# The last 64 tokens of q and k, both heads in one bank, on quarters of the TensorE array

## The chip, the cores and the metric

The kernel runs on one core of one Trainium2 chip. The metric is the device time of one execution in microseconds; a kernel's time is the median of several executions. The profile is one execution, recorded by the hardware. Its engines are PE (TensorE, the matrix array; PEld is its loading of weights), DVE (VectorE), ACT (ScalarE), POOL (GpSimd) and SP (SyncE, which here issues DMAs).

## What is computed

Linear attention, then two feed-forward layers, all in float32. Batch 8, 8 heads, 576 tokens, head size 64, 128 features.

```python
def phi(x):
    proj = np.einsum('bhsd,df->bhsf', x, w_phi)
    proj = proj - np.max(np.abs(proj), axis=-1, keepdims=True)
    return np.concatenate([np.exp(proj), np.exp(-proj)], axis=-1)
q_p, k_p = (phi(q), phi(k))
kv = np.einsum('bhsf,bhsd->bhfd', k_p, v)
z = np.sum(k_p, axis=2)
num = np.einsum('bhsf,bhfd->bhsd', q_p, kv)
den = np.einsum('bhsf,bhf->bhs', q_p, z)[..., None] + 1e-06
x = num / den
...
xk = mu_k * x + (1.0 - mu_k) * x_prev        # xr alike, with mu_r
k = np.maximum(xk @ w_k, 0.0)
x = 1.0 / (1.0 + np.exp(-(xr @ w_r))) * (k * k @ w_v)
...
h = np.maximum(x @ w_in, 0.0)                # then a convolution over 3 tokens
out = h * gate @ w_out                       # gate: sigmoid of the convolution
```

## The kernel before

Attention works on pairs of heads: 8 x 4 = 32 pairs, each with q and k of two heads, head 0 on SBUF partitions 0 to 63 and head 1 on 64 to 127 (tile `rqk`). The 576 tokens of a head are four groups of 128 and a rest of 64. In `rqk` the last 64 columns of q stand right ahead of the last 64 of k, so that one slice of 128 columns holds both rests.

`block(Pi)` (L388) runs once for each pair, in a software pipeline. It does `turn` and `turn_end` for pair Pi (transposes of the centred projections of q, and their exponentials `qf`), `front` for pair Pi + 2 (the projections of the rest of q and k, `rows_last`, and of the rest of k, `rows4`, tile `pk`, with their centring), the projections of q for pair Pi + 1 (`rows4`, tile `pq`), `sums4` (kv and z, tile `pkv`), `results` (tile `pn`, divided into `xn`), and `features` for pair Pi + 2 (the exponentials of k: `kp`, and `kr` for the rest). The output of a pair is transposed into `xT` by `column` (tile `px`) and `column_end` (tile `pr`, which it shares with the transposes of `turn_end`).

Before the change the rest goes so. `rows_last` (L263) takes two PSUM tiles (in the program `p1`, in the trace `p`), one for each head, and makes one product for each: 64 rows of the array (the head's half), 128 columns of weights (the 64 tokens of q, then the 64 of k), 128 features streamed through. `centre` (L282) is a reduce (`mx<-p`) and a subtraction (`t<-p,mx`) on DVE for each head. In the result q's tokens are on partitions 0 to 63 and k's on 64 to 127, so `features` takes `t[64:]` of each head to the head's half of `kr` with four ACT operations, and `turn_end` (L355) transposes the tile of each head, of which it uses the 64 columns of q.

The trace names a matmul's tile as rows*columns of the array: 64*128 for `p`, `pk` and `pq`, 128*64 for `pkv` and `pn`, 128*128 for transposes and the feed-forward products. A float32 product is two passes there, each with its own weight load; a transpose and a float32r product is one.

The order on PE is written out by hand; that of DVE and ACT is set by a scheduler with a model of the timeline. From Pi = 4 (`MS`) on, parts of the first feed-forward layer (`moe`: `psk`, `psr`, `psv`) are put between the blocks on PE; from Pi = 5 the block begins with `px`. After the last pair follow the rest of that layer and the second one (`psh`, `pso`). In the first blocks DVE also rounds the feed-forward weights from float64 (`h`, with an ACT operation ahead).

PSUM has eight banks: a ring of three (`psm`, tag `mm`), from which `rows_last`, part of `pq` and the feed-forward products allocate, and a ring of five (`psa`, tag `at`).

Of the kernel before, what the change touches and what calls it, by code (L numbers as in the profile page):

```python
# [8 lines left out]
F32 = mybir.dt.float32  # L9
F32R = mybir.dt.float32r  # L10
U32 = mybir.dt.uint32
AF = mybir.ActivationFunctionType
# [3 lines left out]
P = 128  # L16
B, H, S, D = 8, 8, 576, 64
NP = H // 2
DM, DFF, FT = 512, 1024, 128
# [23 lines left out]
def fused_kernel(ctx: ExitStack, tc: tile.TileContext, qk, va, wphi, ones2, mu, wk, wv, wr, win, wout, cw, out):  # L43
    nc = tc.nc
    T, SY = nc.tensor, nc.sync
# [23 lines left out]
    V, A, G = Noted(nc.vector), Noted(nc.scalar), Noted(nc.gpsimd)  # L69
# [31 lines left out]
    ident = const.tile([P, P], F32, name="ident")  # L101
    make_identity(nc, ident)
    wp0 = const.tile([P, 2 * FT], F32, name="wp0")
# [50 lines left out]
    psm = ctx.enter_context(tc.tile_pool(name="psm", bufs=PSM, space=bass.MemoryType.PSUM))  # L154


    with ExitStack() as p1:
        pool = p1.enter_context(tc.tile_pool(name="p1", bufs=1))
# [63 lines left out]
        for h in range(2):  # L222
            for w in ((wr, wrh, wrl), (wv, wvh, wvl)):
                n = w[1].shape[1] // 2
# [10 lines left out]
        xk, vts = {}, {}  # L235
# [18 lines left out]
        ts, kps_, kvs = {}, {}, {}  # L254

        def rows(Pi, prods):

            x = xk[Pi]
            for o, h, j in prods:
                r = slice(D * h, D * h + D)  # L260
                T.matmul(o, x[r, j * P:j * P + P], wp0[r, h * FT:h * FT + FT], start=True, stop=True)

        def rows_last(Pi):  # L263
            ps = [psm.tile([P, 512], F32, tag="mm", name="p1") for _ in range(2)]
            ps = [p_[:, :FT].rearrange("p (a n) -> p a n", a=1) for p_ in ps]
            rows(Pi, [(ps[h][:, 0], h, 4) for h in range(2)])
            t = pool.tile([P, 1, 2, FT], F32, tag="t1", bufs=2, name="t")
            for h in range(2):
                centre(ps[h], t[:, :, h])
            ts[Pi] = [t]  # L270

        def rows4(Pi, j0, nm):
# [9 lines left out]
        def centre(ps, t):  # L282
            n = ps.shape[1]
            mx = pool.tile([P, 4], F32, tag="mx", bufs=3, name="mx")[:, :n]
            V.tensor_reduce(mx, ps, axis=AX.X, op=ALU.max, apply_absolute_value=True)
            V.tensor_tensor(t, ps, mx.unsqueeze(2).to_broadcast([P, n, FT]), ALU.subtract)
# [8 lines left out]
        def features(Pi, tk):  # L295
            kp = kps_[Pi] = []
            for h in range(2):
                k_ = pool.tile([P, 4, 2, FT], F32, tag="kp", bufs=2, name="kp")
                A.activation(k_[:, :, 0], tk[h], AF.Exp)
                A.activation(k_[:, :, 1], tk[h], AF.Exp, scale=-1.0)  # L300
                kp.append(k_)

            k_ = pool.tile([P, 2, FT], F32, tag="kr", bufs=1, name="kr")
            for h in range(2):
                r = slice(64 * h, 64 * h + 64)
                A.activation(k_[r, 0], ts[Pi][0][64:, 0, h], AF.Exp)
                A.activation(k_[r, 1], ts[Pi][0][64:, 0, h], AF.Exp, scale=-1.0)
            kp.append(k_)

        def sums4(Pi):  # L310
# [11 lines left out]
        def column(Pi):  # L322

            xn = xns.pop(Pi)
            xt = main.tile([P, 2 + S], F32, tag="xT", bufs=XT, name="xT")
            xT[divmod(Pi, NP)] = xt
            G.memset(xt[:, 0:1], 0.0)
            px = psa.tile([P, 512], F32, tag="at", name="px")
            for j in range(4):
                T.transpose(px[:, j * P:j * P + P], xn[:, j], ident)  # L330
            A.copy(xt[:, 1:513], px)
            return xn, xt
# [20 lines left out]
            return qf, t1  # L353

        def turn_end(qf, t1, pr):  # L355
            for h in range(2):
                T.transpose(pr[:, P + h * P:2 * P + h * P], t1[:, 0, h], ident)
            for h in range(2):
                for c in range(2):
                    A.activation(qf[h][:, c, 512:], pr[:, P + h * P:P + h * P + 64], AF.Exp, scale=1.0 - 2 * c)  # L360

        def results(Pi, qf):

# [20 lines left out]
        def front(Pi):  # L384
            rows_last(Pi)
            return centre4(rows4(Pi, 5, "pk"), "tk")

        def block(Pi):  # L388
# [4 lines left out]
            if Pi >= 0:  # L393
                if Pi > MS:
                    x = column(Pi - 1)
                qf, t1 = turn(Pi)
                pr = psa.tile([P, 512], F32, tag="at", name="pr")
                if Pi > MS:
                    copies = column_end(*x, pr)
                turn_end(qf, t1, pr)  # L400
                if Pi > MS:
                    copies()
# [15 lines left out]
            if nk:  # L418
                features(Pi + 2, tk)
                if Pi + 2 > 1:  # L420
                    load_v(Pi + 2)
# [175 lines left out]
        with tc.manual_schedule(engines={mybir.EngineType.PE}):  # L597
            tk = front(0)
            features(0, tk)
            for Pi in range(-1, B * NP):  # L600
                for n, _ in enumerate(attention(Pi)):
                    extras(Pi, n)
                    feed(Pi)
            x = column(B * NP - 1)
            column_end(*x, psa.tile([P, 512], F32, tag="at", name="px"))()


    with ExitStack() as p2:
        pool = p2.enter_context(tc.tile_pool(name="p2", bufs=1))
# [88 lines left out]
        for g_ in range(0, B * S, 4 * S):  # L698
            a = g_
# [65 lines left out]
```

## Time and profile before

| | |
|---|---|
| median of 3 executions | 1225.81 us (1225.13 to 1226.35) |
| the profiled execution | 1225.83 us, its span 1224.0 us |
| PE busy | 98% of the span |
| DVE busy | 62% |
| ACT busy | 57% |
| the chain that ended last | PE 90%, DVE 5%, ACT 2% |

A busy share is an average over stages: the profile has to be read stage by stage, as the rows further down do. The chain is followed back from the last instruction, at each step to what released it. The length of a matmul in the trace runs from its start to the end that the recorder models, and neighbours overlap; the pace of a group is read from one group's start to the next one's.

### The profile page before, as it was taken

The page shows a single profiled execution, that of the slowest core. Times are in us where ns is not written, and L with a number is a line of the kernel's source. Part 1 is how long each engine was busy: PE and PEld are TensorE (multiplying, and loading weights), DVE is VectorE, ACT ScalarE, POOL GpSimd, SP SyncE. Part 2 cuts the span into 40 slices and gives each one's busy share as a digit, 9 for nine tenths or more (in the row PEclk, how much of TensorE's full clock was granted, in tenths as well). Part 3 has the DMA queues.
Part 4 walks back from the last instruction along what each step waited for, and adds up shares of the span by engine and source line. Part 5 has one row for each costly group of instructions (what it writes and reads, how often), then busy time and mean ns, then how long its engine had stood idle before and what let it go on. Part 6 is the DMA issues. An engine that isn't in the chain of part 4 may idle for free.

```text
span 1224.0 us, 29034 instructions
## 1 busy us (share of the span) xinstructions
PE 1202.0 (98%) x11920; PEld 1135.5 (93%) x11920; DVE 762.1 (62%) x1584; ACT 696.7 (57%) x1644; POOL 86.3 (7%) x213
## 2 busy tenths in 40 slices
PE   7899999999999999999999999999999999999998
PEld 6787999999999999999999999998889888888887
DVE  7989676576675765766656534426555754466555
ACT  6777765566565655665555533325654655455554
POOL 1000001111111111111000000000000000000000
PEclk9999999999999999999999999999999999999999
DMA  6665121223232322332110004050122101210220
GB/s 223 221 218 196 59 80 59 86 93 120 89 93 76 117 83 86 93 121 71 50 42 23 11 21 158 20 188 19 44 63 63 43 21 62 63 53 11 63 62 32
DMA packets 56532, 100.81 MB, mean 82 GB/s; under 512 B 10320, under 2 KB 38608, under 8 KB 56400
## 3 DMA queue, kind: packets, MB, share of 16 engines
q1 hardware_dynamic: 40272, 61.65, 14.8%
q0 software_dynamic: 6768, 27.69, 7.4%
q10 hardware_dynamic: 9360, 9.61, 2.8%
q8 instruction: 94, 1.54, 0.5%
q14 instruction: 38, 0.31, 0.1%
HBM read 66.42 MB, written 27.26 MB: 77 GB/s over the span
## 4 chain that ended last, share of the span: by engine, by line
PE 90%; DVE 5%; ACT 2%; issue 1%; DMA 1%; SPq 0%; ACTq 0%; DVEq 0%
PE psh L150 5%; PE psh L152 5%; PE psh L151 5%; PE psv L150 5%; PE pkv L318 5%; PE psv L151 5%; PE psk L151 5%; PE psv L152 5%; PE psk L152 5%; PE psk L150 5%; PE pso L150 5%; PE pso L151 5%; PE pso L152 5%; PE pn L371 4%; PE psr L150 3%; PE psr L151 3%
## 5 line engine op out<-in xcount | busy, mean ns | idle before, releaser
L58 DVE SCALAR_TENSOR_TENSOR ct<-h,cw,ct 128x460 f32<-128x460 f32 (+2 forms) x160 | 111.4, 696 | 84.6 <-ACT ct L58 83.5
L150 PE MATMUL psv<-kh,wvl 128*128 128x288 f32 x480 | 142.2, 297 | 0.0
L151 PE MATMUL psv<-kl,wvh 128*128 128x288 f32 x480 | 141.9, 296 | 0.0
L151 PE MATMUL psk<-ml,wkh 128*128 128x288 f32 x480 | 141.7, 295 | 0.0
L152 PE MATMUL psk<-mh,wkh 128*128 128x288 f32 x480 | 141.4, 295 | 0.0
L152 PE MATMUL psv<-kh,wvh 128*128 128x288 f32 x480 | 141.1, 294 | 0.0
L150 PE MATMUL psk<-mh,wkl 128*128 128x288 f32 x480 | 140.9, 294 | 0.0
L152 PE MATMUL psh<-xh,wih 128*128 128x462 f32 (+1 forms) x320 | 118.9, 372 | 0.0
L151 PE MATMUL psh<-xl,wih 128*128 128x462 f32 (+1 forms) x320 | 118.8, 372 | 0.0
L151 PE MATMUL pso<-gl,woh 128*128 128x460 f32 (+1 forms) x320 | 117.9, 370 | 0.0
L152 PE MATMUL pso<-gh,woh 128*128 128x460 f32 (+1 forms) x320 | 117.7, 370 | 0.0
L58 ACT ACTIVATE kf<-psk 128x288 f32<-128x288 f32 x128 | 52.2, 408 | 111.5 <-PE psk L152 105.6
L150 PE MATMUL psh<-xh,wil 128*128 128x462 f32 (+1 forms) x320 | 107.3, 372 | 0.0
L58 ACT ACTIVATE h<-psh 128x462 f32<-128x462 f32 (+3 forms) x128 | 47.8, 409 | 76.8 <-PE psh L152 75.6
L150 PEld LDWEIGHTS psv<-kh,wvl 128*128 128x128 f32 x480 | 90.3, 188 | 0.8
L151 PEld LDWEIGHTS psv<-kl,wvh 128*128 128x128 f32 x480 | 90.4, 188 | 0.0
L150 PEld LDWEIGHTS psk<-mh,wkl 128*128 128x128 f32 x480 | 90.2, 188 | 0.1
L151 PEld LDWEIGHTS psk<-ml,wkh 128*128 128x128 f32 x480 | 90.2, 188 | 0.0
L152 PEld LDWEIGHTS psv<-kh,wvh 128*128 128x128 f32 x480 | 90.2, 188 | 0.0
L152 PEld LDWEIGHTS psk<-mh,wkh 128*128 128x128 f32 x480 | 90.2, 188 | 0.0
L58 ACT ACTIVATE kp<-t 128x512 f32<-128x512 f32 x128 | 70.3, 618 | 34.6 <-PE pkv L318 28.9
L58 DVE SCALAR_TENSOR_TENSOR x<-sg,psv 128x288 f32<-128x288 f32 x64 | 29.0, 454 | 97.5 <-PE psv L152 91.4
(108 smaller groups left out, 2822.7 us busy)
## 6 DMA issues: line engine op xcount, KB each, us to landing
rqk<-qk POOLq DMA_DIRECT2D x29, 576.0 KB, 4.8
va<-va POOLq DMA_DIRECT2D x30, 325.0 KB, 4.8
x2s<-x SPq DMA_DIRECT2D x30, 288.0 KB, 2.3
raw<-wk SPq DMA_DIRECT2D x8, 512.0 KB, 5.4
raw<-wv SPq DMA_DIRECT2D x8, 512.0 KB, 4.0
raw<-win SPq DMA_DIRECT2D x16, 256.0 KB, 2.9
raw<-wout SPq DMA_DIRECT2D x16, 256.0 KB, 2.9
x2r<-x2s ACTq DMA_DIRECT2D x16, 231.0 KB, 2.6
```

Source lines behind the costliest of these rows:

```text
L58: x = op(*a, **k)
L150: T.matmul(ps, wl, xh, start=first, stop=False)
L151: T.matmul(ps, wh, xl, start=False, stop=False)
L152: T.matmul(ps, wh, xh, start=False, stop=last)
L318: T.matmul(o[r:r + 64], k_[:, r:r + 64], v_, start=(i == 0), stop=(i == len(prods) - 1))
L371: T.matmul(pn[b_][64 * r:64 * r + 64, j], qf[h_][:, c, o:o + 64], kv[:, c, h_], start=(j == 0 and c == 0), stop=(j == 4 - b_ and c == 1))
```

## The change

The two products of `rows_last` become four, each for one head and one of q and k (`a` = 0 for q, 1 for k), with 64 rows and 64 columns of the array: head 0 on the quarter at rows 0 and columns 0, head 1 on the quarter at rows 64 and columns 64. All four write one PSUM tile: head h on partitions 64 h to 64 h + 63, q in the first 128 columns, k in the next 128. One reduce and one subtraction centre it. `features` then takes both heads in one operation for each sign, and `turn_end` transposes one tile, in which the heads stand side by side.

```diff
         def rows_last(Pi):
-            ps = [psm.tile([P, 512], F32, tag="mm", name="p1") for _ in range(2)]
-            ps = [p_[:, :FT].rearrange("p (a n) -> p a n", a=1) for p_ in ps]
-            rows(Pi, [(ps[h][:, 0], h, 4) for h in range(2)])
-            t = pool.tile([P, 1, 2, FT], F32, tag="t1", bufs=2, name="t")
-            for h in range(2):
-                centre(ps[h], t[:, :, h])
+            x = xk[Pi]
+            ps = psm.tile([P, 512], F32, tag="mm", name="p1")[:, :2 * FT].rearrange("p (a n) -> p a n", a=2)
+            for a in range(2):
+                for h in range(2):
+                    r = slice(D * h, D * h + D)
+                    T.matmul(ps[r, a], x[r, 512 + D * a:512 + D * a + D], wp0[r, h * FT:h * FT + FT], start=True, stop=True)
+            t = pool.tile([P, 2, FT], F32, tag="t1", bufs=2, name="t")
+            centre(ps, t)
             ts[Pi] = [t]
...
             k_ = pool.tile([P, 2, FT], F32, tag="kr", bufs=1, name="kr")
-            for h in range(2):
-                r = slice(64 * h, 64 * h + 64)
-                A.activation(k_[r, 0], ts[Pi][0][64:, 0, h], AF.Exp)
-                A.activation(k_[r, 1], ts[Pi][0][64:, 0, h], AF.Exp, scale=-1.0)
+            A.activation(k_[:, 0], ts[Pi][0][:, 1], AF.Exp)
+            A.activation(k_[:, 1], ts[Pi][0][:, 1], AF.Exp, scale=-1.0)
             kp.append(k_)
...
         def turn_end(qf, t1, pr):
-            for h in range(2):
-                T.transpose(pr[:, P + h * P:2 * P + h * P], t1[:, 0, h], ident)
+            T.transpose(pr[:, P:2 * P], t1[:, 0], ident)
             for h in range(2):
                 for c in range(2):
-                    A.activation(qf[h][:, c, 512:], pr[:, P + h * P:P + h * P + 64], AF.Exp, scale=1.0 - 2 * c)
+                    A.activation(qf[h][:, c, 512:], pr[:, P + h * D:P + h * D + D], AF.Exp, scale=1.0 - 2 * c)
```

On PE, in the block of Pi = 5 (the first in which `px` comes first), the order is this, - before and + with the change. Sizes are those of the weights and of what streams; `wp_74` is `wp0`, and a row with a number behind `p` is the projection of the rest.

```order
 L330 MATMUL px<-ident,xn 128x128 x4
 L350 MATMUL pt<-ident,t 128x128 x8
 L335 MATMUL pr<-ident,xn 128x128
-L357 MATMUL pr<-ident,t 128x128 x2
-L261 MATMUL p_1366<-wp_74,rqk 128x128
-L261 MATMUL p_1367<-wp_74,rqk 128x128
+L356 MATMUL pr<-ident,t 128x128
+L269 MATMUL p_1332<-wp_74,rqk 64x128 x4
 L261 MATMUL pk<-wp_74,rqk 128x128 x8
 L261 MATMUL pq<-wp_74,rqk 128x128 x8
 L318 MATMUL pkv<-va,kp 64x65 x32
```

The place of each group is as it was; between the transposes and `pk` one transpose less and two products more stand. The other blocks differ in the same rows.

On DVE this is the part of the block of Pi = 1 around the centring of the rest, before the change. `h` is a weight that is being rounded.

```order
L58 TENSOR_SCALAR xn<-pn,rd 128x128
L58 TENSOR_SCALAR h<-h 128x512
L58 TENSOR_REDUCE mx<-p_476 128x1
L58 TENSOR_REDUCE mx<-p_477 128x1
L58 TENSOR_SCALAR h<-h 128x512
L58 TENSOR_TENSOR t<-p_476,mx 128x128
L58 TENSOR_TENSOR t<-p_477,mx 128x128
L58 SCALAR_TENSOR_TENSOR h<-raw,h 128x512
```

The same place with the change:

```order
L58 TENSOR_SCALAR xn<-pn,rd 128x128
L58 TENSOR_SCALAR h<-h 128x512
L58 TENSOR_REDUCE mx<-p_462 128x2
L58 TENSOR_SCALAR h<-h 128x512
L58 TENSOR_TENSOR t<-p_462,mx 128x256
L58 SCALAR_TENSOR_TENSOR h<-raw,h 128x512
```

Two reduces became one with two results, and two subtractions one of twice the columns; the neighbours kept their order. In later blocks a few neighbours changed places on DVE and ACT: a `ml<-xf,mh` stands between the two subtractions of `pq`, and a cast of `mh` between the `kp` operations of the two heads.

## Rows read from the trace of the kernel before

**Rows 1.** The page's busy times and, in 40 slices, the clock granted to TensorE

```profile
PE 1202.0 (98%) x11920; PEld 1135.5 (93%) x11920; DVE 762.1 (62%) x1584; ACT 696.7 (57%) x1644; POOL 86.3 (7%) x213
...
PEclk9999999999999999999999999999999999999999
```

**Rows 2.** Stretches: length; busy PE, PEld, DVE, ACT, POOL (instructions); granted clock, DMA share, GB/s

```profile
35.50:47.20 11.70, 9.49 (x195) 8.44 (x196) 11.63 (x29) 9.27 (x25) 1.07 (x2) 1.00 0.66 216
...
82.00:712.00 630.00, 627.57 (x8010) 611.49 (x8009) 420.98 (x941) 378.70 (x966) 70.46 (x110) 1.00 0.26 83
```

**Rows 3.** What PE waited for from 70 to 740 us: us in total, times, longest

```profile
PE psv L484 <- DVE x L58: 0.7, 1, 0.7
PE pq L261 <- ACT qf L58: 0.7, 1, 0.7
PE pn L371 <- DVE t L58: 0.7, 1, 0.7
PE pk L261 <- ACT xT L58: 0.4, 1, 0.4
```

**Rows 4.** PE in order of time, 420.0 to 424.9 us: start, length to last end

```profile
420.24 0.27 PE L335 MATMUL pr<-ident,xn 128*128 128x128 f32 x1
420.35 0.38 PE L357 MATMUL pr<-ident,t 128*128 128x128 f32 x2
420.66 0.49 PE L261 MATMUL p<-wp,rqk 64*128 64x128 f32 x4
420.98 1.06 PE L261 MATMUL pk<-wp,rqk 64*128 64x128 f32 x16
421.88 1.06 PE L261 MATMUL pq<-wp,rqk 64*128 64x128 f32 x16
422.87 2.09 PE L318 MATMUL pkv<-va,kp 128*64 128x65 f32 x64
```

**Rows 5.** PE at 420.62 to 420.66 us alone, in order of time

```profile
420.45 0.27 PE L357 MATMUL pr<-ident,t 128*128 128x128 f32 x1
```

**Rows 6.** Tile `p` from 82 to 740 us: duration ns min/median/max, first and last start

```profile
L261 PE MATMUL p<-wp,rqk x100: 272/322/373, 83.0 to 666.6; 64*128 64x128 f32 x100
```

**Rows 7.** Tile `pkv` from 420 to 430 us, columns as in rows 6

```profile
L318 PE MATMUL pkv<-va,kp x64: 219/222/271, 422.9 to 424.7; 128*64 128x65 f32 x64
```

**Rows 8.** PE in order of time, 28 to 64 us

```profile
29.95 2.09 PE L318 MATMUL pkv<-va,kp 128*64 128x65 f32 x64
31.86 0.61 PE L318 MATMUL pkv<-va,kr 128*64 128x130 f32 x8
32.31 2.27 PE L371 MATMUL pn<-kvf,qf 128*64 128x65 f32 x72
35.52 1.25 PE L350 MATMUL pt<-ident,t 128*128 128x128 f32 x8 [0.95 <-DVE t L58]
...
38.65 1.25 PE L261 MATMUL pk<-wp,rqk 64*128 64x128 f32 x16 [1.23 <-DVE xn L58]
...
62.01 1.25 PE L261 MATMUL pk<-wp,rqk 64*128 64x128 f32 x16 [1.23 <-DVE xn L58]
```

**Rows 9.** DVE in order of time, 33 to 48 us

```profile
37.75 0.76 DVE L58 TENSOR_TENSOR xn<-pn,rd 128x256 f32<-128x256 f32 x2
38.42 0.34 DVE L58 TENSOR_SCALAR xn<-pn,rd 128x128 f32<-128x128 f32 x1
...
39.01 0.48 DVE L58 TENSOR_REDUCE mx<-p 128x1 f32<-128x128 f32 x2
39.41 0.42 DVE L58 TENSOR_SCALAR h<-h 128x512 uint32<-128x512 uint32 x1
```

**Rows 10.** ACT in order of time, 4 to 26 us

```profile
16.83 1.02 ACT L58 ACTIVATE kr<-t 64x128 f32<-64x128 f32 x4
```

**Rows 11.** DVE in order of time, 4 to 26 us

```profile
10.87 1.29 DVE L58 TENSOR_REDUCE mx<-pk 128x4 f32<-128x512 f32 x2 [0.23 <-PE pk L261]
...
21.16 0.43 DVE L58 TENSOR_SCALAR h<-h 128x512 f32<-128x512 f32 x1 [0.51 <-ACT h L58]
```

## The prediction

> **What bounds the kernel now.** I read the page first: PE is busy 98% of the span and the granted clock stands at the top digit in all forty slices [rows 1]. A busy share does not say that PE never waits, so the table of stretches came next [rows 2]. From 82 to 712 us PE is busy 627.6 of 630 us, DVE two thirds of it, ACT three fifths. There an instruction more or less on PE moves the end by its own length. From 35.5 to 47.2 us it is the other way: DVE works 11.63 of 11.70 us and PE 9.49. The list of what PE waited for between 70 and 740 us [rows 3] has four single waits, 2.5 us in all, each for DVE or ACT. So one edit has two prices: on PE in the long stretch, on DVE in the first 70 us, and what it saves on ACT and DVE after that is worth no more than those four waits.
>
> **What one block costs on PE.** I took the block at 420 us, in order of time [rows 4], and the last transpose of it alone [rows 5]. Each float32 product of the program runs as two passes: two products of `p` give x4, eight of `pk` x16. Passes of head 0 and head 1 use different halves of the array's rows and run as a pair, so `pk` needs 421.88 - 420.98 = 0.90 us for eight pairs, 0.1125 us a pair. `p` has two pairs, 0.225 us, but takes 420.98 - 420.66 = 0.32. The other 0.10 is the first load, which nothing covers: the first matmul of `p` takes 373 ns, later ones 272 [rows 6]. Ahead of it the two transposes start at 420.35 and 420.45, 0.10 to 0.11 apart, but `p` starts 0.21 after the second: a change of tile shape (128*128 to 64*128) holds PE for 0.10. From `pq` to `pkv` (64*128 to 128*64) it is alike: 0.99 us instead of 0.90. There the load is half as wide, and the first matmul takes 271 ns instead of 222, so 0.05 for a first load of 64 columns [rows 7].
>
> **The change, part by part.**
>
> The second transpose of `t1` goes: -0.11 us in a block.
>
> The products of the last tokens go from two to four, on 64 by 64 tiles. Does a quarter tile run faster? The trace has no 64*64 tile, but it has tiles half as wide. In `pkv` 64 passes (32 pairs) over 65 columns take 31.86 - 29.95 = 1.91 us, 0.060 a pair; the eight over 130 columns take 0.45 us, 0.1125 a pair [rows 8]. The load was 64 wide in both, so the columns that stream through set the pace, and all passes here stream 128. Four products are eight passes: four pairs at 0.1125 = 0.45 us if the two heads still run together (+0.225), eight single passes = 0.90 us if they don't (+0.675). I take the pairs: pairs on different columns of the array that share a bank (`pkv`) are in the trace, and so are pairs on different rows with a bank each (`pk`). The new pair differs in both, and nothing in these rows says that it must queue.
>
> Tile shapes: 128*128 to 64*64 costs the same 0.10, with a first load of 0.05 instead of 0.10 (-0.05). Then comes a change that was not there, 64*64 to 64*128, ahead of `pk`: 0.09 of standstill and 0.10 for a first load of 128 columns, +0.19. Its bounds are 0, if tiles with the same row split follow each other freely, and 0.20 by the worst row. I take 0.19, since both changes of shape in these rows pay a standstill and a first load. The Trainium skill says the same for the case that no row here shows: "TensorEngine Tiling (Array Packing)", section Key Properties, has the engine drain when the tiling mode changes, and lists 64×64 and 64×128 as modes apart.
>
> Sum of a block: 0.225 - 0.05 + 0.19 - 0.11 = +0.255 us. `p` stands in 25 blocks after 82 us (x100 [rows 6], four passes each): +6.4 us. Two more blocks, the last, only lose a transpose: -0.2.
>
> Centring goes from four DVE ops on 128 columns to two on 256. In the trace two reduces over 128 columns take 39.41 - 39.01 = 0.40 us, and two ops over 256 columns (`xn`) 38.42 - 37.75 = 0.67 [rows 9]. Four times 0.20 becomes two times 0.335: -0.13 us of DVE. It counts where DVE is the bound: PE waits 0.95 us for `t` at 35.52 and 1.23 us for `xn` at 38.65 [rows 8], and both come back in each block until `pk` at 62.01 us, three periods of 11.7 us and the part of a fourth. Four blocks: -0.5. There PE's +0.255 disappears in these waits; without that cover it would be +1.0.
>
> ACT loses two of four `kr` ops, a half of 1.02 us [rows 10]. At 21.16 us DVE waited 0.51 us for an `h` that ACT makes behind them [rows 11]: -0.5. Against that, at 10.87 us DVE waited 0.23 us for PE's `pk` [rows 11], and PE gets there some 0.36 us later, the transpose not being ahead of it yet: +0.4. Net for the start -0.1, and -0.6 for everything before 70 us.
>
> The four waits: PE comes to them up to 0.36 us later within a block, while DVE has 0.13 and ACT 0.5 us less to do. Some will shrink, none should grow; between 0 and -2.5 I take half, -1.2. The order of DVE and ACT differs in a few places (an ACT cast between two pairs of `kp` ops, a `ml` between two `t`), with consumers a block later; I cost it at nothing, covered by that block's time. Without the cover it would be a wait such as the longest above, 0.7 us, in the blocks where it stands. PSUM's `mm` ring loses an allocation in a block, which nothing waited for.
>
> The profiled execution took 1225.83 us (span 1224.0), the median is 1225.81, so one sum serves both: 1225.8 + 6.4 - 0.2 - 0.6 - 1.2 = **1230.2 us**, 0.36% slower. Within 0.2% (2.5 us) a measurement can't tell the two kernels apart.
>
> **Rivals.**
>
> *The heads queue for the bank.* Both heads of a product now write the same bank, from different halves of the rows. If the second waits for the first, `p` has eight passes in a row: 0.45 us more in each of 25 blocks, +11.2, so 1241.4. For it: in the rows before, products on different row halves never share a bank (`p` has two tiles). Against it: the two write different partitions, and column pairs that do so in one bank run together [rows 8]. "TensorEngine Tiling (Array Packing)", section Restrictions and Gotchas, of the Trainium skill states that different row tiles can't access the same PSUM bank at the same time; by that rule the time would be this rival's. I give it 0.16.
>
> *The extra change of shape is free* (the other side). If PE goes from 64*64 to 64*128 without standstill and with its loads ahead, as from `pk` to `pq`, the 0.19 goes: -4.75 us, so 1225.4, no change. It decides as soon as the change costs under 0.11 us instead of 0.19. For it: the row split stays. Against: `pq` to `pkv` and `pr` to `p` both pay [rows 4, 5]. 0.18.
>
> *DVE and ACT were worth more*: all four waits vanish and the start gains twice as much. That is -1.9 us on top, 1228.3 with my PE costs, so still slower, and 1223.5 only together with the free change. And a wait that the new order of ACT adds, as long as the 0.7 us of [rows 3], in half of the 25 blocks would be +9: about 1239. 0.10 for both.
>
> **How the numbers follow.** My case has 0.56, with 1228.3 to 1232 as its own range, and a seventh of it falls under the 2.5 us. Slower: 0.48 + 0.16 + 0.04 = 0.68. Same: 0.08 of mine, 0.14 of the free change, 0.02 of the last: 0.24. Faster: 0.08, the lower edge of the free change and of the last. The range goes from 1224.6, the free change with a little more gain, to 1241.8, the queue for the bank: about 0.14 lie outside.
>
> **What would show it.** In a block near 420 us: one `pr` from `t` instead of two; `p` x8 from first start to `pk` in about 0.59 us with starts in pairs a few ns apart (1.04 and single starts if the heads queue), and the first matmul of `pk` longer than 272 ns (equal if the change is free). DVE's `mx<-p` and `t<-p` 32 times each, at about 0.42 us; `kr` 64 times on 128 partitions. `pk`, now at 62.01 us, some 0.5 us earlier. I am wrong in substance if `p` to `pk` is under 0.45 us, or if PE gets a new wait that comes back in each block.

## The result and the profile after

The changed kernel takes 1233.25 us (median of 6, 1232.98 to 1233.68) against 1225.82 us: 1.0061 of the time, 95% interval 1.0048 to 1.0074. That is 7.4 us slower, where 4.4 were forecast. The profiled execution has a span of 1231.5 us. Its page, busy times and granted clock:

```profile
PE 1211.9 (98%) x12016; PEld 1139.1 (92%) x12016; DVE 761.0 (62%) x1520; ACT 676.4 (55%) x1580; POOL 85.1 (7%) x213
...
PEclk9999999999999999999999999999999999999999
```

ACT lost 20 us of work and DVE 64 instructions, but the share of PE stands at 98% as in [rows 1]: what was taken off two engines that wait came back on the one that doesn't. A block of the long stretch, PE in order of time, which answers to [rows 4] and [rows 5]:

```profile
424.16 0.27 PE L335 MATMUL pr<-ident,xn 128*128 128x128 f32 x1
424.27 0.27 PE L356 MATMUL pr<-ident,t 128*128 128x128 f32 x1
424.48 0.65 PE L269 MATMUL p<-wp,rqk 64*64 64x128 f32 x8
425.06 1.16 PE L261 MATMUL pk<-wp,rqk 64*128 64x128 f32 x16
426.05 1.06 PE L261 MATMUL pq<-wp,rqk 64*128 64x128 f32 x16
427.04 0.63 PE L318 MATMUL pkv<-va,kp 128*64 128x65 f32 x14
```

From `p` to `pk` it is now 425.06 - 424.48 = 0.58 us instead of 0.32, and from `pk` to `pq` 0.99 instead of 0.90. One transpose of 0.11 us is gone. From the first `pr` to `pkv` it is 2.88 us instead of 2.63: +0.25 us, where +0.255 was the sum. Over two blocks without the wait described below, the start of `pkv` goes from 202.64 to 251.58 us before the change and from 203.02 to 252.48 with it, which is 0.26 us more in a block. The matmuls of `p` from 82 to 748 us and those of `pk` in this block (ns min/median/max), for [rows 6]:

```profile
L269 PE MATMUL p<-wp,rqk x200: 269/269/320, 82.3 to 674.0; 64*64 64x128 f32 x100
```

```profile
L261 PE MATMUL pk<-wp,rqk x16: 272/272/373, 425.1 to 425.9; 64*128 64x128 f32 x16
```

The first load of `p` costs 0.05 us (320 against 269), and `pk` has one of 0.10 (373 against 272) that it did not have. So far it is the sum. The rest of the loss is in another place. This is PE at the end of a `psr` group, about 410 us:

```profile
409.56 0.30 PE L151 MATMUL psr<-ml,wrh 128*128 128x288 f32 x1
409.69 0.29 PE L152 MATMUL psr<-mh,wrh 128*128 128x288 f32 x1
410.10 0.37 PE L150 MATMUL psv<-kh,wvl 128*128 128x288 f32 x1
410.30 0.29 PE L151 MATMUL psv<-kl,wvh 128*128 128x288 f32 x1
```

Matmuls follow each other at 0.13 us, but `psv` starts 0.41 us after the last `psr`, and its successor 0.20 after it. DVE in the same microseconds:

```profile
407.99 0.69 DVE L58 TENSOR_TENSOR t<-pq,mx 128x512 f32<-128x512 f32 x1
408.59 0.76 DVE L58 TENSOR_TENSOR ml<-xf,mh 128x576 fp32r<-128x576 f32 x1
409.26 0.69 DVE L58 TENSOR_TENSOR t<-pq,mx 128x512 f32<-128x512 f32 x1
```

The second subtraction of `pq` ends at 409.26 + 0.69 = 409.95, and `psv` starts at 410.10. `psv` is the third tile that the ring of three banks gives out after `pq` of head 1 (two `psr` come between), so it gets that bank and has to wait until DVE has read it. Before the change the two subtractions stood together and ended at 405.98, a quarter of a microsecond ahead of the `psv` that followed at 406.25; DVE and PE of the kernel before:

```profile
404.69 1.29 DVE L58 TENSOR_TENSOR t<-pq,mx 128x512 f32<-128x512 f32 x2
...
405.95 0.76 DVE L58 TENSOR_TENSOR ml<-xf,mh 128x576 fp32r<-128x576 f32 x1
```

```profile
406.25 0.29 PE L150 MATMUL psv<-kh,wvl 128*128 128x288 f32 x1
```

How often the loads of `psv` sat idle for it, by the view of that line from 250 to 620 us:

```profile
  PE psr L152: 2.2, 7
```

Seven times. Each costs 0.41 + 0.20 - 2 x 0.13 = 0.35 us, 2.4 us together. That the view names PE's `psr` is its rule, by which a wait is put down to what came last by the profile; the times above speak for DVE, and e1 below decides it. The other waits of PE between 70 and 748 us are those of [rows 3], three of them shorter by 0.2 to 0.3 us:

```profile
PE psv L483 <- DVE x L58: 0.7, 1, 0.7
PE pq L261 <- ACT qf L58: 0.4, 1, 0.4
PE pn L370 <- DVE t L58: 0.4, 1, 0.4
PE pk L261 <- ACT xT L58: 0.2, 1, 0.2
```

At the start the change gained what was forecast. DVE around the centring of the rest, for [rows 9], and PE's waits for DVE, for [rows 8]:

```profile
38.62 0.42 DVE L58 TENSOR_REDUCE mx<-p 128x2 f32<-128x256 f32 x1
38.96 0.42 DVE L58 TENSOR_SCALAR h<-h 128x512 uint32<-128x512 uint32 x1
39.29 0.42 DVE L58 TENSOR_TENSOR t<-p,mx 128x256 f32<-128x256 f32 x1
```

```profile
35.13 1.25 PE L350 MATMUL pt<-ident,t 128*128 128x128 f32 x8 [0.60 <-DVE t L58]
...
38.26 1.34 PE L261 MATMUL pk<-wp,rqk 64*128 64x128 f32 x16 [1.18 <-DVE xn L58]
...
61.36 1.25 PE L261 MATMUL pk<-wp,rqk 64*128 64x128 f32 x16 [1.18 <-DVE xn L58]
```

The reduce lets the next operation start after 0.34 us, where two took 0.40; the `pk` that stood at 62.01 us stands at 61.36. By the starts of `pk`, 0.05 us were gained up to 27 us, 0.34 in the next period and 0.13 in each of the two after it.

### The profile page after: what moved, and what is told of

It reads as the page before. It is cut to its first block, busy times and chain, and to the rows that moved or that the text cites. A ratio compares the mean times of both kernels' runs of the same rounds, so it can differ in the third digit from the quotient of the medians.

```text
span 1231.5 us, 29070 instructions
## 1 busy us (share of the span) xinstructions
PE 1211.9 (98%) x12016; PEld 1139.1 (92%) x12016; DVE 761.0 (62%) x1520; ACT 676.4 (55%) x1580; POOL 85.1 (7%) x213
## 4 chain that ended last, share of the span: by engine, by line
PE 81%; DVE 11%; issue 3%; ACT 3%; POOL 1%; DMA 1%; SPq 0%; ACTq 0%; POOLq 0%; DVEq 0%
PE psv L150 5%; PE psh L150 5%; PE psh L152 5%; PE psh L151 5%; PE psv L151 5%; PE psv L152 5%; PE pso L150 5%; PE pso L151 5%; PE pso L152 5%; PE psk L151 4%; PE psk L152 4%; PE psk L150 4%; PE pkv L318 4%; PE pn L370 3%; DVE t L58 2%
```

## The experiments

All times are medians on the device, ratios against the kernel before on the same chip, with a 95% interval. All these kernels compute the whole reference.

| run | us | ratio |
|---|---|---|
| e1, changed kernel, `ml` behind | 1230.49 | 1.0038 (1.0023 to 1.0053) |
| e3, products twice | 1235.22 | 1.0076 (1.0061 to 1.0091) |
| e8, e3 with `ml` behind | 1231.30 | 1.0042 (1.0028 to 1.0056) |
| e4, a bank for each head | 1245.54 | one execution, no ratio |
| e5, quarters for 7 pairs | 1225.61 | 0.9998 (0.9988 to 1.0007) |
| e6, stacked by DVE | 1236.20 | 1.0084 (1.0069 to 1.0099) |
| e7, e6 with an order on DVE | 1226.56 | 1.0004 (0.9995 to 1.0013) |
| e9, before with that order | 1226.09 | 1.0002 (0.9993 to 1.0011) |
| e10, rest after `pk` | 1226.84 | 1.0010 (1.0001 to 1.0019) |
| e11, order for late mixes | 1226.44 | 1.0007 (0.9998 to 1.0015) |
| e12, stacked from pair 12 on | 1223.84 | 0.9983 (0.9974 to 0.9992) |
| e13, e12 with quarters for 7 pairs | 1223.54 | 0.9979 (0.9970 to 0.9988) |

**The new wait (e1).** A dependency without a semaphore, on DVE's own order:

```diff
+                lastq[0] = V.last          # after the centring of pq in block
...
-                V.tensor_tensor(lo[:, c0:c0 + 2], xf, f(hi[:, c0:c0 + 2]), ALU.subtract)
+                ml = V.tensor_tensor(lo[:, c0:c0 + 2], xf, f(hi[:, c0:c0 + 2]), ALU.subtract)
+                tc.add_manual_dep(ml.ins, lastq[0].name, ...)
```

> The changed kernel, with the two `ml` subtractions of the mix set behind the second subtraction of `pq` on DVE; nothing else differs. Theory (the new wait of `psv` comes from the order of DVE, which lets an `ml` of 0.67 us in ahead of the operation that frees the bank of `pq`): the seven waits of about 0.34 us go, -2.4 us, near 1230.9, and PE's block keeps its 0.585 us from `p` to `pk`. Rival (the ring of three banks has one allocation less in a block, so `psv` comes to the bank of `pq` too early whatever the order): the waits stay, near 1233.2.

1230.49 us, 2.76 less than the changed kernel, with 2.4 expected; the spans of the two profiled executions, 1229.1 and 1231.5 us, differ by 2.4. DVE of this kernel in the corresponding block:

```profile
406.89 1.28 DVE L58 TENSOR_TENSOR t<-pq,mx 128x512 f32<-128x512 f32 x2
...
408.09 0.75 DVE L58 TENSOR_TENSOR ml<-xf,mh 128x576 fp32r<-128x576 f32 x1
```

The same view of the loads, from 250 to 620 us, has no idle time left. The ring is as in the changed kernel, so the ring alone is not the cause: the scheduler's order is. What remains, 1230.5, is near the forecast 1230.2, though not every term of it was as forecast (see below).

**Stream and change of shape (e3, e8).** The kernel before, each product of the rest made twice:

```diff
-            rows(Pi, [(ps[h][:, 0], h, 4) for h in range(2)])
+            rows(Pi, [(ps[h][:, 0], h, 4) for _ in range(2) for h in range(2)])
```

> The kernel before, with the two products of the rest made twice over (the same tiles of 64 rows and 128 columns, the same result): four pairs of passes as in the change, but no change of tile shape ahead of `pk`. Theory (stream and shape change are two terms): from `p` to `pk` 0.55 us instead of 0.325, the last pair of `p` 0.105 us ahead of `pk`, no first load in `pk`: +0.225 us in each of 25 blocks, +5.6, near 1231.4. Rival (the standstill comes with the number of passes, or `pk` waits for something else): the last pair of `p` 0.2 us ahead of `pk` and its first matmul at 373 ns, near 1236.

PE in order of time:

```profile
426.06 0.71 PE L261 MATMUL p<-wp,rqk 64*128 64x128 f32 x8
426.61 1.06 PE L261 MATMUL pk<-wp,rqk 64*128 64x128 f32 x16
427.50 1.06 PE L261 MATMUL pq<-wp,rqk 64*128 64x128 f32 x16
```

0.55 us from `p` to `pk` and 0.89 from `pk` to `pq`: twice the passes cost 0.225 us, and without a change of shape `pk` keeps its pace. As many passes as the quarters have, and no standstill: it belongs to the shape. The time was a miss, 1235.2 instead of 1231.4. The list of waits has a new one:

```profile
PE psv L150 <- DVE rd L58: 2.0, 7, 0.3
```

The scheduler answered this edit too, which touches PE alone, by an order with an `ml` between the two subtractions of `pq`, and `psv` waits seven times. Here the ring gives out two tiles for the rest in each block, as before the change, so the wait does not need the ring's missing allocation. The list counts idle time alone; by the starts of `pkv` each of the seven blocks is 0.5 to 0.6 us longer than in e8, 3.8 us in all. So e8, the same with the dependency of e1:

> The kernel with the products of the rest made twice (e3), with `ml` behind the second subtraction of `pq`. Theory: the waits of `psv` go and what is left is the stream alone, +0.225 us in 25 blocks, near 1231.2. Rival (the extra 3.9 us of that kernel have another cause): above 1233.

1231.30 us, 5.4 above the kernel before on the same chip (1225.88), where 5.6 was counted. In its trace the start of `pkv` falls back by 4.56 us over the 21 blocks from 153 to 673 us, 0.22 in a block: that is the stream.

**Do the heads queue for the bank? (e4)**

```diff
-            ps = psm.tile([P, 512], F32, tag="mm", name="p1")[:, :2 * FT].rearrange(...)
+            ps = [psm.tile([P, 512], F32, tag="mm", name="p1")[:, :2 * FT].rearrange(...) for _ in range(2)]
```

> The changed kernel with a PSUM bank for each head: the same quarters, the centring in four operations on 64 partitions. Theory (the heads run together in one bank already): `p` to `pk` stays at 0.585 us in the long stretch, with starts in pairs; the time is above the changed kernel's, since DVE has more to do. Rival (one bank makes the heads queue in part): `p` to `pk` shorter by 0.1 us or more.

```profile
434.96 0.65 PE L269 MATMUL p<-wp,rqk 64*64 64x128 f32 x8
435.54 1.16 PE L261 MATMUL pk<-wp,rqk 64*128 64x128 f32 x16
436.54 0.72 PE L261 MATMUL pq<-wp,rqk 64*128 64x128 f32 x10
```

0.58 us with two banks, 0.58 with one: the heads don't queue. Each of its four DVE operations, on 64 partitions and 256 columns, takes 0.42 us, as long as one on 128 partitions in the changed kernel. The time of its single execution, 1245.5 us, was not taken apart: its start is slower by 4.8 us than the changed kernel's (`pkv` of pair 5 at 69.10 us instead of 64.33), and after that `pn` waits 2.2 us once and `psv` eight times, 4.1 us in all, for DVE. How much of this is the longer centring and how much the scheduler's order is not shown.

**Where the loss is (e5).** The changed code for the first seven pairs, that of before for the others, in `rows_last`, `features` and `turn_end`:

```diff
+            if Pi < 7:
                 x = xk[Pi]
...
+            else:
+                ps = [psm.tile([P, 512], F32, tag="mm", name="p1") for _ in range(2)]
...
```

> Quarters, one centring and one transpose for the first seven pairs only (those whose rest is taken before 70 us), the way of before for the other 25. Theory: the start gains what it gained in the changed kernel (the first feed-forward product at 68.9 us instead of 69.5) and the long stretch is as before: -0.6 us, near 1225.2. Rival (the loss of the changed kernel is not in the 25 blocks but follows from the start, where DVE and PE get another phase): 1228 or more.

1225.61 us: no loss, so the whole of it is in the 25 later blocks. But no gain either, though the first feed-forward product starts at 69.17 us instead of 69.53: the wait of `pn` for DVE near 109 us grows from 0.7 to 1.2 us and takes back what the start gave. The changed kernel has the same code for these seven pairs and reached that product at 68.89 us, so the start's gain also hangs on the order around it.

**One transpose without quarters (e6, e7, e9).** The products as before, and the heads set one above the other by DVE, which may write other partitions than it reads:

```diff
+            for h in range(2):
+                mx = ...
+                V.tensor_reduce(mx, ps[h], axis=AX.X, op=ALU.max, apply_absolute_value=True)
+                for a in range(2):
+                    i, o = slice(D * a, D * a + D), slice(D * h, D * h + D)
+                    V.tensor_scalar(t[o, a], ps[h][i], mx[i], None, ALU.subtract)
```

> For the last 25 pairs the products of before (two tiles of 64 rows and 128 columns, two banks), but centred by four subtractions on 64 partitions that put the heads one above the other, so that one transpose and two `kr` operations do; the first seven pairs as in the changed kernel. Theory (PE's count decides in the long stretch): a transpose of 0.11 us less in 27 blocks, -3.0, and -0.6 at the start: near 1222.2. Rival (DVE, with two operations and some 0.4 us more in a block, frees a bank too late for PE, as in the changed kernel): waits of 0.1 to 0.4 us come back in 7 to 25 blocks, 1224 to 1230.

1236.2 us, past the rival's upper end. DVE has much more than 0.4 us more in a block: the four subtractions alone took 1.45 us, where the two of before take 0.28 each. In order of time:

```profile
454.65 1.45 DVE L58 TENSOR_SCALAR t<-p,mx 64x128 f32<-64x128 f32 x4
```

PE's waits show where most of it went:

```profile
PE pn L382 <- DVE t L58: 4.8, 9, 3.0
PE psv L150 <- DVE rd L58: 4.0, 8, 0.5
```

e7 takes the broadcast operand and sets both operations of the mix behind `pq`; e9 has the two dependencies alone, on the kernel before:

```diff
-                    V.tensor_scalar(t[o, a], ps[h][i], mx[i], None, ALU.subtract)
+                    V.tensor_tensor(t[o, a], ps[h][i], mx[i].to_broadcast([D, FT]), ALU.subtract)
...
+                    tc.add_manual_dep(xs.ins, lastq[0].name, ...)       # xf
...
+                tc.add_manual_dep(ml.ins, lastq[0].name, ...)
```

> The stacked kernel (e6) with two things mended on DVE: the four subtractions take the maxima as a broadcast operand, as in the kernel before, and the mix's `xf` and `ml` operations stand behind the second subtraction of `pq`. Theory (what the stacked kernel lost came from DVE alone, through the banks that it frees for `pn` and `psv`): those waits go, PE has one transpose of 0.11 us less in 27 blocks: 1222 to 1223, under the kernel before. Rival (DVE has too much to do in a block in any order): waits of `pn` or `psv` for DVE in more than three blocks, 1226 or more.

1226.56 us: 9.6 less than e6, but not under the kernel before. The waits of `psv` for the bank of `pq` are gone; the one near 120 us, where DVE also rounds weights, grew from 0.7 to 2.4 us. The two edits were not tried apart.

> The kernel before with the mix's `xf` and `ml` operations behind the second subtraction of `pq`, nothing else. Theory: no `psv` waits there before, so the order alone is worth nothing: 1225.0 to 1226.5. Rival (the order by itself gains, and a gain of the stacked kernel would be its): under 1224.

1226.09 us: the order alone gains nothing, as the theory had it. But it moves waits: that of `pn` near 109 us is gone, and the one of `psv` near 120 us grew from 0.7 to 1.8 us, with no operation added on DVE:

```profile
PE psv L488 <- DVE x L58: 1.8, 1, 1.8
```

**Two misses (e10, e11).** e11 is e7 with the first of these lines, e10 has both edits:

```diff
+                if Pi >= 8:
                     lastq[0] = V.last
...
-            return centre4(rows4(Pi, 5, "pk"), "tk")
+            tk = centre4(rows4(Pi, 5, "pk"), "tk")
+            if stack:
+                stack()                 # the four subtractions
+            return tk
```

> The stacked kernel with the order on DVE (e7), but that order only for mixes after the block of Pi = 8, and the centring of the rest behind that of `pk` for the last 25 pairs. Theory (each wait of PE goes when the operation that frees its bank comes earlier on DVE): the wait of 2.4 us for a `psv` near 120 us falls to 0.7 as before the change, and the waits of `pn` for the first `pk` bank, 0.16 us in every second block, go too; PE keeps one transpose of 0.11 us less in 27 blocks: 1223 to 1224, under the kernel before. Rival (the rest then comes too late, and `psr` waits for its banks): waits of `psr` for DVE, 1226 or more.

1226.84 us, neither. From about 180 us on the theory holds: no wait of `pn` or `psv` comes back, and each block is some 0.1 us shorter. The wait near 120 us is as long as in e7, and `pk` waits twice for ACT, 1.4 us near 104 us and 0.5 near 155:

```profile
PE psv L510 <- DVE x L58: 2.6, 1, 2.6
PE pk L261 <- ACT xT L58: 1.9, 2, 1.4
```

> As e7, with the order on DVE only for mixes after the block of Pi = 8; the centring of the rest stays ahead of that of `pk`. Theory: only the wait of `psv` near 120 us goes back to 0.7 us, -1.7: near 1224.8, between e7 and e10. Rival (that wait is DVE's load, not the order): 2.4 us there as in e7, near 1226.5.

1226.44 us: the long wait is now one of `pn`.

```profile
PE pn L382 <- DVE t L58: 2.7, 1, 2.7
```

In three kernels with three orders it moved, and stayed as long. From 70 to 110 us DVE of the kernel before is busy 35.84 of 40 us, against 273 of 400 from 200 to 600. I read that as no room for two more operations there, whatever the order; that is argued from the load, and the order that would avoid it was not found. Against it stands e9, where an order alone made 1.8 us of such a wait.

**A version that is faster than both (e12, e13).** So the way of before for pairs 0 to 11 and e10's for the other 20:

```diff
+            if Pi < 12:                 # in rows_last: as before the change
...
-                if Pi >= 8:
+                if Pi >= 10:
                     lastq[0] = V.last
```

> The way of before for pairs 0 to 11; for the last 20 pairs the products of before, stacked by four subtractions behind the centring of `pk`, one transpose and two `kr` operations, with the order on DVE for mixes after the block of Pi = 10. Theory (in the long stretch DVE has room for two operations more if they come after what PE waits for, and between 70 and 150 us, where weights are still rounded, it has not): as before up to 200 us, then 0.09 to 0.12 us less in each block, some 22 blocks and the last two transposes: -2.3, near 1223.5, faster than before. Rival (the load on DVE comes back as waits wherever the change begins): a new wait of 1 us or more at the first stacked block, 1225 or more.

1223.84 us, 0.17% under the kernel before. That is less than the 0.2% which the prediction took as the limit of a measurement; the interval lies below 1, and the trace shows where the gain is. The start of `pkv` in two blocks, of e12:

```profile
202.64 2.09 PE L339 MATMUL pkv<-va,kp 128*64 128x65 f32 x64
...
666.74 2.09 PE L339 MATMUL pkv<-va,kp 128*64 128x65 f32 x64
```

The kernel before has the first of them at 202.64 us too, and the second here:

```profile
668.58 2.09 PE L318 MATMUL pkv<-va,kp 128*64 128x65 f32 x64
```

So it is nothing until 202.64 us, and then 1.84 us over 19 blocks, 0.10 in a block, which is the transpose.

> As e12, with the changed kernel's quarters for pairs 0 to 6. Theory: the 0.6 us that they gain before 70 us are lost again at the wait of `pn` near 109 us, as in the run with quarters for the first seven pairs alone: no faster than e12, 1223.3 to 1224.2. Rival (that loss was an accident of the order): 1222.9.

1223.54 us. Its wait of `pn` is 1.1 us instead of 0.7, so a part of the start's gain is lost again, but in its trace `pkv` still starts 0.36 us ahead of e12's at 666.74 us. The medians differ by 0.30 us and the intervals of the ratios overlap: the times do not tell the two apart.

## Why the prediction came out as it did

The direction and the range were right; the likeliest time was 3.0 us too low. The measured 1233.25 us lies above 1228.3 to 1232, the range of the prediction's own case, and inside the whole range only because that reaches up to 1241.8 for heads that queue for the bank, which they did not do. That it lies inside is luck. By the steps of the prediction:

- *The block on PE, +0.255 us, +6.4 in all.* Right, with 0.25 to 0.26 measured, and right term by term: 0.45 us for four pairs (e4 says the heads run together, e3 and e8 price the added pairs), a first load of 0.05, and 0.19 for the change to 64*128 ahead of `pk`. The rule on modes in "TensorEngine Tiling (Array Packing)", section Key Properties, of the Trainium skill agrees with the trace here: between a 64×64 and a 64×128 tile PE stood still. Both rivals on PE fall. The rule on row tiles and a PSUM bank in the Trainium skill, "TensorEngine Tiling (Array Packing)", section Restrictions and Gotchas, does not hold for these two tiles, which write different partitions of the bank: 0.58 us with one bank and with two. Products on 64*128 tiles of both heads into one bank, which would write the same partitions, were not tried.
- *The start, -0.6.* Measured -0.65, `pk` at 61.36 instead of 62.01. The 0.13 us of a block came as counted in two periods and 0.34 in the one before them, where four times 0.13 were forecast; e5, with the same code, gained 0.36 in all up to the first feed-forward product. The sum is closer than its parts.
- *The four waits, -1.2.* Of the three that shrank, those of `pn`, `pk` and `pq` gave 0.2 to 0.3 us each, some 0.7 in all; the one of `psv` near 119 us kept its 0.7. This term was too large by 0.5 us.
- *The order of DVE and ACT, "I cost it at nothing, covered by that block's time".* This is the step that failed: it cost 2.4 us. I looked for who reads the result of the delayed operation, and that is a block away. I did not ask who waits for the bank that it reads. The second subtraction of `pq` frees the bank that `psv` takes; before the change it ended a quarter of a microsecond ahead of `psv`, and the `ml` that came in between takes 0.67. The text named such a wait as a rival, but on ACT, and gave it 0.10 together with its opposite. It also named as a sign of being wrong in substance a new wait of PE that comes back in each block: it came back, in seven of the 25.

The sum of what was measured, with 25 times 0.26 us on PE and 0.2, as forecast, for the last transposes: 6.5 + 2.4 - 0.65 - 0.7 - 0.2 = 7.35 us, against 7.4.

## What to carry to other kernels

A product cut into quarters of the array is no cheaper if as many columns stream through each: look at what streams, not at how much of the array is used, and count each change of tile shape with the first load behind it. Here two of the four quarters were in use at a time, where two 64*128 tiles cover the whole array; so twice the products took twice the time. Where one engine is busy without a break, operations saved on others are worth the waits that they end, and no more. When an edit lets a scheduler choose a new order, ask of each operation that moves whose bank or buffer it frees; the reader of its result may be far off while the next owner of its input is already there.

## What the runs showed of the hardware

Two matmuls on quarters that share neither rows nor columns run at the same time into one PSUM bank: in the trace of the changed kernel the two passes of a pair start within 0.01 us of each other and a pair takes 0.11 us, four of them 0.45; in e4, with a bank for each head, it is the same.

A long wait can cost more than its length. In e10, after PE had been idle for 2.61 us up to 121.79 us, the granted clock from 123 to 127 us was 0.61 on the mean, so that for most of that stretch it was at the lower level of 1.2 GHz; from 127 us it was full again. The columns are length, busy times of PE, PEld, DVE, ACT and POOL, clock, DMA share and GB/s:

```profile
123.00:127.00 4.00, 4.00 (x12) 2.92 (x11) 3.67 (x6) 2.25 (x5) 0.00 (x0) 0.61 0.68 236
127.00:131.00 4.00, 4.00 (x18) 3.16 (x17) 1.05 (x2) 0.00 (x0) 0.00 (x0) 1.00 0.00 0
```

In the profiled execution of e11 a wait of 2.7 us had no such fall behind it, so the length of the wait alone does not decide it here. One kernel can have it both ways: of the 11 executions of e11 the three with a mean granted clock of 1.000 took 1225.17 to 1225.69 us, the eight at 0.998 or less 1226.24 to 1228.39. So a part of what e11 lost in its median is the clock's, and e7's executions divide alike, six at 0.999 (1225.58 to 1226.56) and five at 0.998 (1226.68 to 1227.16). That their fall, too, stood behind the long wait is not shown, since one execution of each was profiled.
